# Sigmoid attention and routed tokens: a DRAM-to-DRAM output copy, a reset of the bank order, and a reordered last batch

## The chip, the cores and the metric

The kernel runs on one core of a Trainium2 chip. Its engines are TensorE (PE, matrix products; PEld is its weight load), VectorE (DVE), ScalarE (ACT), GpSimd (POOL) and SyncE (SP, which here issues DMAs and does nothing else). Sixteen DMA engines serve the core. The metric is the device time of one execution in microseconds (us); smaller is better.

## What is computed

Eight batches, 12 heads, 448 tokens, head size 64. First comes attention with a sigmoid in place of the softmax. Its result, laid out as 448 rows of 768 numbers for each batch, goes into a layer in which only 128 of the 448 tokens are routed through two matrix products; the others pass unchanged.

```python
scores = scale * np.matmul(q, k.transpose(0, 1, 3, 2)) - np.log(S)
attn = 1.0 / (1.0 + np.exp(-scores))
x = np.matmul(attn, v)                 # (B,H,S,D) -> (B, S, H*D)
...
scores = np.einsum('bsd,d->bs', x, w_gate)
out = x.copy()
for b in range(B):
    top_idx = np.argpartition(-scores[b], capacity)[:capacity]   # 128 rows
    xe = x[b, top_idx]
    ye = np.maximum(xe @ w1, 0.0) @ w2                           # F = 1024
    g = 1.0 / (1.0 + np.exp(-scores[b, top_idx]))
    out[b, top_idx] = x[b, top_idx] + g[:, None] * ye
```

So every row of `out` is either a row of `x`, or a row of `x` plus a gated product. All numbers are float32.

## The kernel before

The 96 pairs of batch and head are worked in groups of 4 heads, 3 groups to a batch, and in 12 stages `s` of two groups. A stage has 7 units `n`. A unit (`unit`, L193) is 32 matmul instructions into two PSUM tiles and two sigmoid activations on ScalarE. Between the units, `gap(s, n)` (L442) places everything else by hand: the whole kernel stands under a manual schedule, so program order is the order on each engine and each queue, and the semaphores follow from what reads and writes what.

- **PSUM.** Four tiles of two banks: a pool `psc` of two, which the units use, and `ps_o[0]` and `ps_o[1]`. `banks("o")` (L82) flips `turns[0]` and takes that one of the two; `banks("any")` alternates between `psc` and `o`. The attention outputs of a stage use both: `outs[s] = [banks(0), banks(1)]` (L233). After the last part of the products with V, at unit 2 of the next stage, `take` (L259) transposes them out of PSUM on VectorE into `x_b`, four instructions, first both halves of tile 0 and then both of tile 1 (L255 to L257).
- **Rows to DRAM.** When a batch's third group has been taken, `gates` (L435) calls `store(b)` (L280) at unit 2 (even batches) or 3 (odd ones). It writes `x_b` twice, with four DMAs each: into a DRAM table `x_d` (two buffers), and into `out[b]`. `x_b` holds 32 columns of a head to a piece, so that these DMAs move pieces of 128 bytes.
- **Routing.** `spread`, `rank` and `place` find the 128 chosen tokens. `select` and `fetch` (L334, L341), a stage later, turn them into a list of rows (`row`, `idx`, two buffers each) and gather these rows from `x_d` into `xe` by an indirect DMA on POOL (L349). `turn_rows` (L354) transposes them on TensorE. Then follow six routed groups in the list `ready`: three `ffn1` (36, 36 and 24 matmuls, Relu by ScalarE into `hT`) and three `ffn2` (16 matmuls, a third of the columns each, VectorE adds them into `xe`). The last `ffn2` scatters `xe` over `out` with an indirect DMA on POOL (L390). Its destination is named as the whole of `out`, so it is ordered behind every write of `out` that stands before it in the program, and every later write of `out` behind it.
- **Where they go.** `go` pops one group from `ready`; `gap` calls it at units 3, 4 and 5. `late` holds what is due at a place (`put`, `due`); `beside` holds the selects.
- **The end.** Stage `NS` = 12 has only gaps. Batch 6 is chosen, five gaps run, three more groups are popped, batch 7 is chosen (`choose(B - 1)`, L504), the rest of `ready` is popped (L505), and then come `turn_rows` and the six groups of batch 7.

SP issues in program order the loads of q and k (`load`, L90), of v (`load_v`, L100), the weights, and the stores.

Of the kernel before, what the change touches and what calls it, by code (L numbers as in the profile page):

```python
# [17 lines left out]
def kernel(  # L18
# [11 lines left out]
    nc = tc.nc  # L30

    B, H, S, Dh = q.shape
# [4 lines left out]
    TT = 32  # L37
    TB = S // TT
# [35 lines left out]
    turns = [0, 0]  # L74
# [15 lines left out]
    def load(i):  # L90

        if i >= NQ:
            return
        raws[i] = [raw.tile([P, TB * Dh], F32, name=f"raw_{nm}") for nm in "kq"]
        for t, src in zip(raws[i], (k, q)):
            nc.sync.dma_start(
                out=t, in_=bass.AP(tensor=src.tensor, offset=src.offset + i * 4 * S * Dh,
                                   ap=[[TB * Dh, P], [1, TB * Dh]]))
# [76 lines left out]
    def turn(i):  # L175


        if i >= NQ:
            return
        kT[i] = head.tile([P, 2, TB, TT], F32, name="kT")  # L180
        qT[i] = head.tile([P, 2, TB, TT], F32, name="qT")
        sk, sq = [t.rearrange("p (r e d) -> p e r d", e=2, d=TT) for t in raws.pop(i)]
        for e in range(2):
            nc.vector.transpose(kT[i][:, e, :HK],  # L184
                                sk[:, e, :HK].rearrange("p (m c) d -> p c m d", c=NF))
        nc.vector.transpose(kT[i][:, :, HK:], sk[:, :, HK:])
        if i == 0:
            for e in range(2):
                nc.vector.transpose(qT[i][:, e], sq[:, e])
        else:  # L190
            nc.vector.transpose(qT[i], sq)  # L191
# [33 lines left out]
    x_tiles, gate_parts, st = {}, {}, {}  # L225
    def values(s, n):

        tv, th = raw_v[s]
        if n == 0:
            outs[s] = [banks(0), banks(1)]  # L233
        o = outs[s]
        first = (0, 2, 2, 0)[n]
        quads = [(first + m) % 4 for m in range(4)]
        work = [(r, c) for c in range(NF) for r in quads]
        if n < 2:
            at = 4 * (NF - 1)
            work[at:at] = [(r, None) for r in quads]  # L240
        for r, c in work:
            x, pr = divmod(r ^ n, 2)
            rows = slice(r * TT, (r + 1) * TT)
            for j in range(2):
                if c is None:
                    w, a = th[rows, 2 * pr + j, :], attn[s, pr, NF]
                else:
                    w = tv[rows, 4 * x + 2 * pr + j, c * Dh:(c + 1) * Dh]
                    a = attn[s, pr, (NF + 1) * x + c]
                nc.tensor.matmul(o[x][j * Dh:(j + 1) * Dh, pr, :S], w, a[rows, j, :],  # L250
                                 start=(n == 0 and c == 0), stop=(n == 3 and c == NF - 1))
        if n < 3:
            nc.scalar.activation(o[x][Dh:Dh + 1, pr, S:S + 1], bias_s[Dh:Dh + 1], AF.Copy)  # L253
        else:
            for x in range(2):  # L255
                for pr in range(2):
                    take(s, pr, x)  # L257
# [11 lines left out]
    def gate_part(i):  # L269
        b, g = divmod(i, NG)  # L270
        tmp = moe.tile([P, TB, 2 * TT], F32, name="scr")
        nc.vector.tensor_tensor(  # L272
            out=tmp,
            in0=x_tiles[b][:, :, 2 * g:2 * g + 2, :].rearrange("p r h d -> p r (h d)"),
            in1=wg_b[:, 2 * g:2 * g + 2, :].rearrange("p (o h) d -> p o (h d)", o=1)
            .to_broadcast([P, TB, 2 * TT]),
            op=ALU.mult)
        nc.vector.tensor_reduce(out=gate_parts[b][:, :, g], in_=tmp, axis=AX.X, op=ALU.add)  # L278

    def store(b):  # L280
        x_d = dram.tile([S, D], F32, name="x_d")
        st[b] = dict(x_d=x_d)
        for dst in (x_d, out[b]):
            view = dst.rearrange("(t r) (h a d) -> a t r h d", r=TB, a=4, d=TT)
            for a in range(4):
                nc.sync.dma_start(out=view[a], in_=x_tiles[b][a * TT:(a + 1) * TT])

    def gate(b):
        g = moe.tile([P, TB], F32, name="gate_s")
        nc.vector.tensor_reduce(out=g, in_=gate_parts[b], axis=AX.X, op=ALU.add)  # L290
        diag = moe.tile([P, TB, TT], F32, name="rep")
        nc.vector.tensor_tensor(
            out=diag,
            in0=iden_t.rearrange("p (o t) -> p o t", o=1).to_broadcast([P, TB, TT]),
            in1=g.rearrange("p (r o) -> p r o", o=1).to_broadcast([P, TB, TT]), op=ALU.mult)
        st[b]["diag"] = diag
# [37 lines left out]
    def select(b, s0, n, pk):  # L334

        tg = tok_gate[b % 2]
        for c in range(NC):
            nc.tensor.matmul(pk[:n, 0:2], sel[:, c, s0:s0 + n], tg[:, c, :],
                             start=(c == 0), stop=(c == NC - 1))
# [56 lines left out]
    ready = []  # L396
# [7 lines left out]
    def go(where="o"):  # L404
        if ready:
            fn, args = ready.pop(0)
            fn(*args, where)

    late = {}
    beside = {}  # L410

    def put(where, s, n, fn, *args):
        where.setdefault((s, n), []).append((fn, args))

    def due(where, s, n):
        for fn, args in where.pop((s, n), []):
            fn(*args)

    def routed(b):

        s = (NG * b + NG - 1) // 2 + 1
        put(late, s, 5 if b == 0 else 4, spread, b)
        for c in range(NC - 1):
            put(late, s, 6 if b == 0 else 4, rank, b, c)
        put(late, s, 6, rank, b, NC - 1)
        put(late, s, 6, place, b)
        if s == NS:
            return
        for s0, n in SLOTS:
            if s + 1 < NS:  # L430
                put(beside, s + 1, 1 if b == 0 else 0, select, b, s0, n)
            put(late, s + 1, 3, turn_rows, b, n)
            put(late, s + 1, 3, routed_groups, b, n)

    def gates(i):  # L435
        gate_part(i)
        b, g = divmod(i, NG)
        if g == NG - 1:
            store(b)
            gate(b)  # L440

    def gap(s, n):  # L442
        if n < 3 and s > 0:
            values(s - 1, n + 1)
            if n == 2:
                gates(2 * s - 2)
        if 3 <= n < NU - 1:
            if not ready:
                due(late, s, n)
            go("any" if s == NS else "o")  # L450
            if n == NU - 2 and s < NS - 2 and len(ready) > 1:
                go()
        if n == NU - 1 and s < NS:
            values(s, 0)
        due(late, s, n)
        if n == 3 and s > 0:
            gates(2 * s - 1)

    def stream():
        for b in range(B):  # L460
            routed(b)
        load(0)
        load(1)
        nc.vector.memset(sel, 0.0)
        nc.vector.memset(bias_s, NEG_LOG_S)
        turn(0)
        load(2)
        load_v(0)
        warm = banks(1)
        for _ in range(3):  # L470
            nc.tensor.matmul(warm[:, 0], sel[:, 0, :], sel.rearrange("p c n -> p (c n)"),
                             start=True, stop=True)
        constants()
        for s in range(NS):
            for n in range(NU):
                unit(s, n)
                if n == (0 if s == 0 else 1):
                    turn(2 * s + 1)
                    load(2 * s + 3)
                if n == 0:  # L480
                    load_v(s + 1)
                    load_weights(5 * s - 5, 5 * s)
                if s == 0 and n == 1:
                    nc.vector.tensor_reduce(
                        out=iden_t, in_=iden.rearrange("p (a t) -> p t a", t=TT),
                        axis=AX.X, op=ALU.add)
                gap(s, n)
                if n == NU - 2:
                    turn(2 * s + 2)
                    load(2 * s + 4)  # L490

        def choose(b):
            for s0, n in SLOTS:
                pk = banks("psc")[:, 0]
                select(b, s0, n, pk)
                fetch(b, s0, n, pk)

        choose(B - 2)
        for n in range(5):
            gap(NS, n)  # L500
        for n in range(3):
            go("any")
        due(late, NS, NU - 1)
        choose(B - 1)  # L504
        while ready:  # L505
            go("any")
        for s0, n in SLOTS:
            turn_rows(B - 1, n, "any")
            routed_groups(B - 1, n)
        while ready:  # L510
            go("any")
        assert not late and not beside
# [32 lines left out]
```

## Time and profile before

| | us |
|---|---|
| time, median of 3 runs | 503.19 (501.88 to 513.16) |
| the profiled execution, its own time | 502.38 |
| its span, first to last instruction | 500.6 |
| PE busy in it | 473.4 (95%) |
| DVE, ACT, POOL busy | 211.8, 189.3, 28.0 |
| mean granted TensorE clock | 0.986 of full speed |
| DMA queue of SP, share of 16 engines' span | 55.9% |

The profile is of one execution. A row of a timeline gives the start and the length in us, the engine, the line of the kernel, the operation, what it writes and reads, the number of instructions merged into the row, and in brackets how long the engine had been idle before it and what released it. The start of one row of matmuls to the start of the next is the pitch: matmuls overlap, and their lengths add up to more than the time they take.

### The profile page before, as it was taken

How to read it: one execution, taken by the hardware profiler on the slowest of the kernel's cores; microseconds unless marked ns; L12 is line 12 of the kernel's file. 1: busy time of each engine (PE TensorE's matmuls, PEld its weight loads, DVE VectorE, ACT ScalarE, POOL GpSimd, SP SyncE). 2: the span in 40 equal slices, each digit the busy share in tenths (PEclk: the TensorE clock that was granted, in tenths of full speed). 3: DMA queues.
4: the chain of work that ended last, by engine and by line, in shares of the span. 5: the costliest groups of instructions: out<-in, count | busy, mean ns of one | idle time of the engine just before them, and what ended most of it. 6: DMA issues, size and time to landing. Idle time of an engine off the chain costs nothing. (4 is left out here: it accounts for less than half of the span.)

```text
span 500.6 us, 14613 instructions
## 1 busy us (share of the span) xinstructions
PE 473.4 (95%) x6662; PEld 307.7 (61%) x6662; DVE 211.8 (42%) x461; ACT 189.3 (38%) x253; POOL 28.0 (6%) x45
## 2 busy tenths in 40 slices
PE   8998999599999999999999999999999999996995
PEld 3564646476477465576467476567565475685894
DVE  4324295526351167345343066257154146470101
ACT  4754464232542543442533442444443443000010
POOL 8000000000000000010000000010000000000100
PEclk9998999799999999999999999999999999999899
DMA  8929198898791097898453098597650077284100
GB/s 268 224 70 352 51 317 128 174 306 132 156 211 75 20 198 128 196 206 133 127 130 106 5 202 130 145 232 121 157 148 33 3 116 118 49 129 98 56 8 31
DMA packets 203421, 68.67 MB, mean 137 GB/s; under 512 B 182048, under 2 KB 194400, under 8 KB 203360
## 3 DMA queue, kind: packets, MB, share of 16 engines
q1 hardware_dynamic: 201952, 61.36, 55.9%
q0 software_dynamic: 1408, 6.39, 4.1%
q8 instruction: 52, 0.85, 0.8%
q14 instruction: 9, 0.07, 0.0%
HBM read 42.57 MB, written 25.17 MB: 135 GB/s over the span
## 5 line engine op out<-in xcount | busy, mean ns | idle before, releaser
L220 ACT ACTIVATE attn<-psc,bias_s 128x896 f32<-128x896 f32 x158 | 151.1, 1003 | 129.8 <-PE psc L209 116.4
L209 PE MATMUL psc<-qT,kT 32*64 32x448 f32 x2528 | 149.4, 545 | 1.4 <-ACT attn L220 1.4
L250 PE MATMUL o<-attn,raw_v 32*64 32x448 f32 x2304 | 133.9, 539 | 0.8 <-ACT o L253 0.8
L209 PEld LDWEIGHTS psc<-qT,kT 32*64 32x64 f32 x2528 | 60.1, 132 | 62.1 <-issue 41.3
L250 PEld LDWEIGHTS o<-attn,raw_v 32*64 32x64 f32 x2304 | 58.8, 133 | 50.3 <-issue 41.9
L375 PEld LDWEIGHTS o<-xeT,w_sb 128*128 128x128 f32 x672 | 78.8, 197 | 12.9 <-issue 6.4
L375 PE MATMUL o<-xeT,w_sb 128*128 128x128 f32 x672 | 81.6, 282 | 3.1 <-DVE x_b L265 2.2
L384 PE MATMUL o<-w_sb,hT 128*128 128x256 f32 x304 | 70.4, 386 | 4.3 <-DVE x_b L265 4.3
L265 DVE STREAM_TRANSPOSE x_b<-o 128x448 f32<-128x448 f32 x48 | 26.9, 617 | 109.2 <-PE o L250 86.7
L384 PEld LDWEIGHTS o<-w_sb,hT 128*128 128x128 f32 x304 | 57.1, 192 | 21.0 <-PE psc L209 7.3
L184 DVE STREAM_TRANSPOSE kT<-raw_k 128x384 f32<-128x384 f32 x48 | 24.7, 553 | 29.0 <-PE psc L209 15.9
L386 DVE SCALAR_TENSOR_TENSOR xe<-o,gate,xe 128x256 f32<-128x256 f32 x19 | 9.2, 483 | 55.4 <-PE o L384 55.4
L377 ACT ACTIVATE hT<-o 128x384 f32<-128x384 f32 (+1 forms) x21 | 9.5, 454 | 57.2 <-PE o L375 57.2
L250 PE MATMUL o<-attn,raw_h 32*64 32x448 f32 x384 | 26.4, 535 | 0.0
L278 DVE TENSOR_REDUCE gate_p<-scr 128x14 f32<-128x896 f32 x24 | 26.1, 1087 | 0.8
L272 DVE TENSOR_TENSOR scr<-x_b,wg_b 128x896 f32<-128x896 f32 x24 | 25.6, 1066 | 0.1
L191 DVE STREAM_TRANSPOSE qT<-raw_q 128x896 f32<-128x896 f32 x23 | 24.7, 1073 | 1.2 <-DMA raw_q<-in_q_dram 1.2
L349 POOL DMA_INDIRECT xe<-x_d,row x8 | 7.9, 988 | 297.0 <-DVE idx L345 221.2
L384 PE MATMUL psc<-w_sb,hT 128*128 128x256 f32 x80 | 19.4, 395 | 4.5 <-ACT hT L377 4.5
L322 DVE SCALAR_TENSOR_TENSOR scr<-rep,tok_gate,earlier 128x448 f32<-128x448 f32 (+1 forms) x32 | 21.8, 682 | 1.1
L319 DVE TENSOR_SCALAR_CACHE_REDUCE scr<-rep,tok_gate 128x448 f32<-128x448 f32 (+1 forms) x32 | 21.4, 669 | 0.9
L307 DVE STREAM_TRANSPOSE scr<-o 128x448 f32<-128x448 f32 x8 | 5.2, 650 | 37.2 <-ACT rep L305 37.2
(54 smaller groups left out, 199.9 us busy)
## 6 DMA issues: line engine op xcount, KB each, us to landing
raw_k<-in_k_dram SPq DMA_DIRECT2D x24, 448.0 KB, 5.0
raw_q<-in_q_dram SPq DMA_DIRECT2D x24, 448.0 KB, 5.5
x_d<-x_b SPq DMA_DIRECT2D x32, 336.0 KB, 7.2
out_dram<-x_b SPq DMA_DIRECT2D x32, 336.0 KB, 6.8
raw_v<-in_v_dram SPq DMA_DIRECT2D x48, 192.0 KB, 4.4
w_sb<-in_moe_w_dram SPq DMA_DIRECT2D x6, 512.0 KB, 5.9
w_sb<-in_moe_w_dram SPq DMA_DIRECT2D x8, 384.0 KB, 4.7
raw_h<-in_v_dram SPq DMA_DIRECT2D x48, 32.0 KB, 4.5
```

The source lines that it names most:

```text
L184: nc.vector.transpose(kT[i][:, e, :HK], sk[:, e, :HK].rearrange("p (m c) d -> p c m d", c=NF))
L191: nc.vector.transpose(qT[i], sq)
L209: nc.tensor.matmul(psc[h // 2][y * Dh:(y + 1) * Dh, h % 2, :S], kT[2 * s + x][d, e, r:r + 2, :].rearrange("d r t -> d (r t)"), qT[2 * s + ...
L220: nc.scalar.activation(a, psc[pr][:, :, :S], AF.Sigmoid, bias=bias_s, scale=QK_SCALE)
L250: nc.tensor.matmul(o[x][j * Dh:(j + 1) * Dh, pr, :S], w, a[rows, j, :], start=(n == 0 and c == 0), stop=(n == 3 and c == NF - 1))
L265: nc.vector.transpose(x_tiles[b][:, :, 2 * g + pr, :], outs[s][x][:, pr, :S].rearrange("p (r t) -> p r t", t=TT))
L272: nc.vector.tensor_tensor(out=tmp, in0=x_tiles[b][:, :, 2 * g:2 * g + 2, :].rearrange("p r h d -> p r (h d)"), in1=wg_b[:, 2 * g:2 * g + 2 ...
L278: nc.vector.tensor_reduce(out=gate_parts[b][:, :, g], in_=tmp, axis=AX.X, op=ALU.add)
L319: nc.vector.tensor_scalar(out=junk[:n], in0=rep[:n], scalar1=own, scalar2=0.0, op0=ALU.is_gt, op1=ALU.add, accum_out=above[:n, c:c + 1])
L322: nc.vector.scalar_tensor_tensor(out=junk[:n], in0=rep[:n], scalar=own, in1=earlier[:n, c, :], op0=ALU.is_equal, op1=ALU.mult, accum_out=l ...
L375: nc.tensor.matmul(ps[:, f - f0, :n], w1_sb[:, t, f * P:(f + 1) * P], xeT[:, t, :n], start=(t == 0), stop=(t == KD - 1))
L384: nc.tensor.matmul(ps[:n, :ND], st[b]["hT"][:, t, :n], w2_sb[:, t, cols], start=(t == 0), stop=(t == KF - 1))
```

## The change

There are four edits. `store` writes only the table `x_d`. A new `copy_out(b)` copies the whole table of a batch into `out[b]` by one DMA, DRAM to DRAM, on SP; it is put at unit 1 of stage 3 for batch 0, at unit 6 of the stage of the store for batches 1 to 6, and right behind `choose(B - 1)` for batch 7. `gap` sets `turns[0]` to 1 at unit 2 of each stage after the first, so that the next `banks("o")` takes tile 0. At the end, the last group of batch 6 (its third `ffn2`, with the scatter) stands behind `turn_rows` of batch 7 rather than ahead of it.

```diff
     def store(b):
         x_d = dram.tile([S, D], F32, name="x_d")
         st[b] = dict(x_d=x_d)
-        for dst in (x_d, out[b]):
-            view = dst.rearrange("(t r) (h a d) -> a t r h d", r=TB, a=4, d=TT)
-            for a in range(4):
-                nc.sync.dma_start(out=view[a], in_=x_tiles[b][a * TT:(a + 1) * TT])
+        view = x_d.rearrange("(t r) (h a d) -> a t r h d", r=TB, a=4, d=TT)
+        for a in range(4):
+            nc.sync.dma_start(out=view[a], in_=x_tiles[b][a * TT:(a + 1) * TT])
+
+    def copy_out(b):
+        nc.sync.dma_start(out=out[b], in_=st[b]["x_d"])
...
         put(late, s, 6, place, b)
         if s == NS:
             return
+        put(late, *((s + 1, 1) if b == 0 else (s, 6)), copy_out, b)
...
             values(s - 1, n + 1)
             if n == 2:
+                turns[0] = 1
                 gates(2 * s - 2)
...
         due(late, NS, NU - 1)
         choose(B - 1)
-        while ready:
+        copy_out(B - 1)
+        while len(ready) > 1:
             go("any")
         for s0, n in SLOTS:
             turn_rows(B - 1, n, "any")
```

## Rows read from the trace of the kernel before

**Rows 1.** The page: busy time of each engine, share of the span, instructions.
```profile
PE 473.4 (95%) x6662; PEld 307.7 (61%) x6662; DVE 211.8 (42%) x461; ACT 189.3 (38%) x253; POOL 28.0 (6%) x45
```

**Rows 2.** Waits of PE: line, released by; us in total, times, longest.
```profile
PE o L359 <- DMA xe<-x_d,row: 4.7, 1, 4.7
PE psc L384 <- ACT hT L377: 4.5, 1, 4.5
PE o L384 <- DVE x_b L265: 4.3, 4, 1.1
PE o L375 <- DVE x_b L265: 2.2, 2, 1.1
```

**Rows 3.** Timeline of VectorE and PE, one of the six waits on L265.
```profile
173.36 2.24 DVE L265 STREAM_TRANSPOSE x_b<-o 128x448 f32<-128x448 f32 x4 [12.91 <-PE o L250]
...
175.75 2.92 PE L375 MATMUL o<-xeT,w_sb 128*128 128x128 f32 x24 [1.09 <-DVE x_b L265]
```

**Rows 4.** Timeline of PE, the last 65 us.
```profile
435.10 0.82 PE L359 MATMUL o<-iden,xe 128*128 128x128 f32 x6
435.75 3.62 PE L384 MATMUL o<-w_sb,hT 128*128 128x256 f32 x16
...
455.58 2.76 PE L384 MATMUL psc<-w_sb,hT 128*128 128x256 f32 x12
...
473.75 4.29 PE L375 MATMUL psc<-xeT,w_sb 128*128 128x128 f32 x36 [0.64 <-ACT xeT L362]
...
488.03 3.62 PE L384 MATMUL psc<-w_sb,hT 128*128 128x256 f32 x16
491.48 3.62 PE L384 MATMUL o<-w_sb,hT 128*128 128x256 f32 x16
```

**Rows 5.** Timeline of VectorE, POOL and ScalarE around the last routing.
```profile
446.94 0.48 DVE L386 SCALAR_TENSOR_TENSOR xe<-psc,gate,xe 128x256 f32<-128x256 f32 x1
...
453.00 0.16 DVE L343 CAST row<-psc 128x1 int32<-128x1 f32 x1 [3.18 <-PE psc L338]
...
459.04 0.99 POOL L390 DMA_INDIRECT out_dram<-xe,idx  x1 [34.99 <-DMA out_dram<-x_b]
462.10 0.16 DVE L345 TENSOR_SCALAR idx<-psc 128x1 int32<-128x1 f32 x1 [8.94 <-DMA out_dram<-xe,idx]
...
462.42 0.38 ACT L377 ACTIVATE hT<-o 128x256 f32<-128x256 f32 x1
```

**Rows 6.** SP's timeline, stores of batch 7; below, their landing from issue.
```profile
434.08 8.87 SPq L286 DMA_DIRECT2D x_d<-x_b  x4
442.99 10.56 SPq L286 DMA_DIRECT2D out_dram<-x_b  x4
...
DMA to landing us min/median/max: 6.4/6.5/7.6
```

**Rows 7.** Timelines of SP, POOL and PE, batch 0; then stretch, busy, PEclk, DMA.
```profile
69.12 13.39 SPq L286 DMA_DIRECT2D x_d<-x_b  x4
...
88.15 1.11 POOL L349 DMA_INDIRECT xe<-x_d,row  x1 [75.78 <-DMA x_d<-x_b]
...
93.88 1.41 PE L359 MATMUL o<-iden,xe 128*128 128x128 f32 x6 [4.66 <-DMA xe<-x_d,row]
...
93.90:101.00 7.10, 6.20 (x29) 5.80 (x30) 1.33 (x3) 0.81 (x1) 0.00 (x0) 0.52 0.89 207
```

**Rows 8.** Line L349, all eight gathers: from issue to landing.
```profile
DMA to landing us min/median/max: 3.8/5.5/6.6
```

**Rows 9.** Busiest stretch of the DMA engines: last two columns, DMA share and GB/s.
```profile
43.00:47.00 4.00, 4.00 (x63) 1.97 (x55) 0.40 (x1) 1.36 (x2) 0.00 (x0) 0.60 1.02 417
```

**Rows 10.** Timeline of POOL: gather of batch 2, scatter of 1, gather of 3.
```profile
198.80 0.98 POOL L349 DMA_INDIRECT xe<-x_d,row  x1 [50.52 <-DVE idx L345]
215.15 1.58 POOL L390 DMA_INDIRECT out_dram<-xe,idx  x1 [15.38 <-DVE xe L386]
238.93 0.97 POOL L349 DMA_INDIRECT xe<-x_d,row  x1 [22.20 <-DVE idx L345]
```

## The prediction, made before the result was seen

> **What bounds the kernel.** I read the page first: PE is busy 473.4 of 500.6 us, and no other engine comes to half the span [rows 1]. The kernel is bound by TensorE, and a change that takes no matmul away can win only the 27.2 us in which PE stands idle, and the time for which its clock is down. DMA traffic, which this change cuts most, wins nothing by itself: what counts is a wait of PE that ends with a DMA. So the second view is PE's waits. Four lines of it hold 15.7 us [rows 2]: one wait of 4.7 us for a gather, one of 4.5 us for ScalarE's `hT`, and six of 1.1 us for the transposes at L265. The rest of the idle time is the start, the end (from 495.1, the end of the last matmul, to 500.6; [rows 4]) and small waits. The timelines then say what stands behind each of the three kinds, and in the windows I looked for clock loss behind them.
>
> **Bank order (`turns[0] = 1`).** The four transposes of a stage take 2.24 us, so a pair takes 1.12, and tile 0's pair comes first. In the stage shown they start at 173.36: tile 0 is free at 174.48, tile 1 at 175.60. PE was ready at 175.75 - 1.09 = 174.66 and had to wait for tile 1 [rows 3]. Had its first routed group asked for tile 0, it would have found it free 0.18 us before it was ready; the small delay behind a semaphore (0.15 us here, 175.60 to 175.75) about eats that, so the wait comes to 0 and not below. This pattern stands six times (stages 5, 6, 7, 9, 10 and 11), 4.3 + 2.2 = 6.5 us [rows 2]. In the other stages the flip happened to stand right already. What is late next: the stage's second request goes to tile 1, which is free 1.0 us after PE's new start (175.60 against 174.66); it comes after the first group, 16 matmuls or more, 3.45 us at the shortest (the pitch in rows 4). So nothing follows, and I take **-6.5 us**. Bounds: 0 if the wait merely moves, -6.5 if it goes.
>
> **The end of the kernel.** Here the second store costs time. Follow rows 5 backwards. PE stops within the first `ffn2` of batch 6, for `hT`. The third part of `hT` is written by ScalarE only at 462.42, since it stands there behind the gate activation of `fetch(7)`, which needs `idx` on VectorE. That was ready to go at about 453.2, behind the cast at 453.00, but waited 8.94 us: it overwrites the buffer of batch 5, which the scatter of batch 5 still reads. The scatter's data were ready at 446.94 + 0.48 = 447.4, but it is ordered behind all earlier writes of `out`, and the store of `out[7]` (four DMAs, issued from 442.99 to 453.55, landing 6.4 to 7.6 us after their issue [rows 6]) was one of them. Hence POOL starts only at 459.04, and `idx` follows 3.06 us later at 462.10 [rows 5].
>
> After the change the write of `out[7]` stands behind `choose(7)` in the program. The scatter of batch 5 goes at 447.5 and has landed at about 450.6, ahead of the cast at 453.00; `idx`, gate and `hT` are not held. Then the last group of batch 6 stands behind `turn_rows(7)`, and its 3.46 us of matmuls cover the eviction for which PE waits 0.64 us now (the row at 473.75). In sum: from the start of the first `ffn2` (455.58) to the start of batch 7's `ffn1` (473.75) it takes 18.17 us now. The same matmuls at undisturbed pitch are three `ffn2` at 491.48 - 488.03 = 3.45 and one `turn_rows` at 435.75 - 435.10 = 0.65 us, together 11.0 [rows 4]. That takes in the stall of 4.5, the 0.64, and the half-speed clock after the stall. **-7.1 us.**
>
> **The copies.** One copy reads and writes 1.376 MB. No DRAM-to-DRAM transfer is in the trace. Its bounds: at the rate of the busiest stretch, 417 GB/s [rows 9], 3.3 us; at that of the four stores it replaces, 10.56 us of issue plus 6.5 of landing [rows 6], 17 us. Its rows are 3 KB, nearer to the loads of that stretch than to pieces of 128 bytes; reading and writing DRAM both count, so I double the lower one and add 3 for the landing: about 9 us, an estimate.
>
> [...]
>
> Each copy adds two waits on SP: for the landing of its `x_d`, and for earlier scatters. Behind it on SP stand loads of v, q and k for a stage later, which already wait for buffers. Each copy also adds a wait on POOL: the next scatter must see it landed. The tightest of these in mid-kernel is the copy of batch 2 (put a few us ahead of the gather at 198.80) against the scatter at 215.15 [rows 10], 16 us or more. For batch 7, SP reaches the copy when `x_d` has landed (issue over at 442.95, so about 449.5 at the latest) and the scatter of batch 5 has (450.6): the copy runs from about 451 to 460. What waits for it is the scatter of batch 6, now due at about 467, and behind it that of batch 7 at 495.9 - 7.1 = 488.8. I take 0 for the copies.
>
> What the copy may hold up is `fetch(7)`, which issues at about 453.4. A gather takes 3.8 to 6.6 us, the most beside loads and stores [rows 8]; it lands between 457.2 and 460. `turn_rows(7)` comes after two more `ffn2`, at 455.58 + 6.9 = 462.5. Slack 2.5 us at worst: 0.
>
> **Batch 0.** [...] PE was ready at 89.22. The stores of `x_d(0)` are unchanged, and end at 82.5; landing at 6.4 at best after the last issue (about 79.9) would free the gather at about 86.5, against 88.15. Beside it then run the loads of group 8 and of v, now earlier by the 11 us of the second store, in its place. So the gather lands between 86.5 + 3.8 = 90.3 and 88.15 + 6.6 = 94.8, against 93.8: a gain of 3.5 to a loss of 1. Nearer to today's than to a free queue, so I take **-1.0 us**; the clock falls as now.
>
> **Sum.** 502.38 (the profiled execution's own time) - 6.5 - 7.1 - 1.0 = 487.8. The median of the runs is 0.8 above that execution, so I say **488 us**, 3.0% less. What a measurement can tell from no change is about 2%, here 10 us: the line is 493.1.
>
> **Rivals.**
> - *The gather of batch 0 escapes.* If it lands by 90.3, the wait falls to 1.1 us, a length after which none of the six shows more than its wait. Then also the clock stays: 7.1 us at 0.52 lose 3.4. 487.8 + 1.0 - 3.6 - 3.4 = 481.8; at most about 480.5. For it: the 128-byte pieces behind `x_d` go. Against: loads take their place. Chance 0.08.
> - *The copy of batch 7 holds up `fetch(7)`.* With the copy at its upper price the two share the engines until 451 + 17 = 468, and `turn_rows(7)` waits up to 5.5 us from 462.5, with about 1.6 us of lower clock behind it: up to 7.1 back, 489 to 495. Decides when the gather needs over 9.1 us. Against: 6.6 is the longest seen. Chance 0.13.
> - *The bank waits stay.* If a tile's release counts the reads of both tiles, or another user takes tile 0 first, 6.5 comes back: 494. Against: PE's start 0.15 us behind the fourth transpose in rows 3, and stages without the wait. Chance 0.09.
> - *Slower: the copy runs on one DMA engine.* One sixteenth of 417 is 26 GB/s, 53 us a copy. Batch 2's would run from about 195 to 248, the scatter of 1 to 252, and VectorE, in order, would hold at `idx` of the gather now at 238.93, some 13 us and PE about 10 of them; the same at batch 4. At the end 451 + 53 = 504, then two scatters in a row, 3 and 4.7 us to the end of the span: 512 for 500.6, less the 7.5 gained before, plus 20 and the 1.8 outside the span, about 526. It decides only where a copy takes over some 34 us (485 for the scatter of 6, to be out of the way at 488.8), so not at two engines, 26 us. For it: no row shows such a transfer; against: SP's loads keep all sixteen engines busy (share 1.02 in rows 9). Chance 0.05.
>
> [...]
>
> **Chances.** Forecast 0.65 (486 to 490 by itself), rivals as given. Leaving out the slower one and most of the unforeseen, the range is 480.5 to 495. Faster by over 2%: 0.65 + 0.08 + half of the held gather, 0.79. Within: the rest of that and the bank rival, 0.16. Slower: 0.05.
>
> **What would show it.** Right: no wait of PE on L265 at the routed groups; POOL's scatter of batch 5 within a us of VectorE's `xe`; no wait of PE on `hT`, no clock below full in the last 40 us; `ffn1` of batch 7 about 7 us closer to the first `ffn2`; a wait on the first gather of 3 to 4.7 us still there. Wrong: copies that land later than 17 us after issue; a wait of PE at `turn_rows(7)`; POOL waiting for `out`<-`x_d`.

## The result: 2.5% faster, with a loss at one place where a gain was forecast

The changed kernel takes 489.85 us (median of 4 runs, 488.26 to 490.36), the kernel before beside it 502.53. The ratio is 0.9749, with a 95% interval of 0.9712 to 0.9787. The forecast was 488, with a range of 480.5 to 495. The profiled execution took 489.37 us, with a span of 487.6 for 500.6: 13.0 us less. Ratios here and below compare fast runs alone; one run of the kernel before (513.16 us) and one of the first experiment (974.12 us) were slow ones and are not in them.

The page of the changed kernel, busy times, clock, DMA traffic and the new copies; the last row gives KB and us from issue to landing (for one of the eight copies, the only one whose landing this profile has):

```profile
PE 470.9 (97%) x6662; PEld 309.5 (63%) x6662; DVE 211.7 (43%) x461; ACT 189.4 (39%) x253; POOL 28.0 (6%) x45
...
PEclk9999999789999999999999999999999999999999
...
DMA packets 117277, 68.67 MB, mean 141 GB/s; under 512 B 95648, under 2 KB 108000, under 8 KB 116960
...
q1 hardware_dynamic: 115808, 61.35, 49.0%
...
out_dram<-x_d SPq DMA_DIRECT2D x8, 1344.0 KB, 9.0
```

TensorE does the same 6662 matmuls. What fell is its idle time, from 27.2 to 16.7 us, and, by 2.5 us, its busy time, which is longer where the clock is low: in the window 43 to 46.5 us, shown below, 48 matmuls fill the 3.5 us at a granted clock of 0.54 and 81 at 1.00 (the mean over the span was 0.986 before and is 0.988 here). DMA packets fell by 42% (203421 before), which by itself, as the third experiment shows (128045 packets, ratio 1.0025), shortens the run by nothing. PE's waits, to be laid beside [rows 2]:

```profile
PE o L361 <- DMA xe<-x_d,row: 5.9, 1, 5.9
PE psc L209 <- ACT attn L220: 1.9, 2, 1.4
...
PE o L377 <- ACT xeT L367: 0.9, 1, 0.9
...
```

The six waits on L265 and the wait for `hT` are gone. The wait for the first gather is not only still there, it grew from 4.7 to 5.9 us.

**Bank order.** The stage of [rows 3] in the timelines of VectorE and PE:

```profile
173.12 2.24 DVE L265 STREAM_TRANSPOSE x_b<-o 128x448 f32<-128x448 f32 x4 [12.88 <-PE o L250]
...
174.45 2.92 PE L377 MATMUL o<-xeT,w_sb 128*128 128x128 f32 x24
```

The group starts 1.33 us after the first transpose, when the first pair (1.12 us) is out and the second is not; before, it started 2.39 us after it. No idle time stands beside the row.

**The end.** Timelines of PE, POOL, VectorE, ScalarE and SP, to be laid beside [rows 4 to 6]:

```profile
428.33 8.86 SPq L285 DMA_DIRECT2D x_d<-x_b  x4
...
441.19 0.48 DVE L388 SCALAR_TENSOR_TENSOR xe<-psc,gate,xe 128x256 f32<-128x256 f32 x1
...
441.95 0.99 POOL L392 DMA_INDIRECT out_dram<-xe,idx  x1 [23.55 <-DVE xe L388]
...
445.01 0.53 SPq L288 DMA_DIRECT2D out_dram<-x_d  x1
...
447.33 0.15 DVE L347 TENSOR_SCALAR idx<-psc 128x1 int32<-128x1 f32 x1
447.68 0.97 POOL L351 DMA_INDIRECT xe<-x_d,row  x1 [4.75 <-DVE idx L347]
...
449.84 3.62 PE L386 MATMUL psc<-w_sb,hT 128*128 128x256 f32 x16
...
450.04 0.38 ACT L379 ACTIVATE hT<-o 128x256 f32<-128x256 f32 x1 [2.29 <-PE o L377]
...
460.86 4.18 PE L377 MATMUL psc<-xeT,w_sb 128*128 128x128 f32 x36
```

The scatter of batch 5 goes 0.3 us after its data; `idx` follows the cast at once; the last part of `hT` is begun 0.2 us after the first `ffn2` and done at 450.42, before that `ffn2` comes to it. From that `ffn2` to batch 7's first `ffn1` it takes 460.86 - 449.84 = 11.02 us, for 18.17 before.

**Batch 0.** Timelines of SP, POOL and PE, and the window behind the wait (PE busy, PEclk, DMA share, GB/s), to be laid beside [rows 7]:

```profile
67.77 13.41 SPq L285 DMA_DIRECT2D x_d<-x_b  x4
81.70 2.17 SPq L96 DMA_DIRECT2D raw_k<-in_k_dram  x1
...
86.12 1.81 SPq L115 DMA_DIRECT2D raw_v<-in_v_dram  x4
...
86.54 1.11 POOL L351 DMA_INDIRECT xe<-x_d,row  x1 [74.18 <-DMA x_d<-x_b]
...
85.57 1.95 PE L209 MATMUL psc<-qT,kT 32*64 32x448 f32 x32
93.42 1.51 PE L361 MATMUL o<-iden,xe 128*128 128x128 f32 x6 [5.90 <-DMA xe<-x_d,row]
...
102.39 1.76 PE L209 MATMUL psc<-qT,kT 32*64 32x448 f32 x32
...
93.40:101.00 7.60, 6.68 (x31) 0.51 1.06 406
```

In the place of the second store, loads of k, q, v and `w2` run beside the gather. It lands 6.7 us after its issue, at 93.3, where it took 5.6 us in the kernel before; and the clock is low behind the wait, 0.51 for 0.52 there.

**Where the 13.0 us lie.** Two units frame batch 0. For the kernel before they, and a window 50 us earlier, stand here:

```profile
87.27 1.94 PE L209 MATMUL psc<-qT,kT 32*64 32x448 f32 x32
...
102.61 1.76 PE L209 MATMUL psc<-qT,kT 32*64 32x448 f32 x32
...
43.00:46.50 3.50, 3.50 (x48) 0.54 1.02 417
```

And the same window of the changed kernel:

```profile
43.00:46.50 3.50, 3.50 (x81) 1.00 1.03 414
```

| stretch, us | before | changed | difference |
|---|---|---|---|
| start to the unit ahead of `turn_rows(0)` | 87.27 | 85.57 | -1.70 |
| from it to the unit behind the first `ffn1` | 15.34 | 16.82 | +1.48 |
| from there to the first `ffn2` of the end | 352.97 | 347.45 | -5.52 |
| from it to `ffn1` of batch 7 | 18.17 | 11.02 | -7.15 |
| from there to the end of the span | 26.85 | 26.74 | -0.11 |

The first row is not what the change was made for. 1.7 us of it are the clock in the window 43 to 46.5: from a unit at 36 us to one at 62 us it takes 26.51 us before (36.01 to 62.52) and 24.82 in the changed kernel (36.45 to 61.27). This goes with the execution and not with the edit: the first experiment, on the changed kernel, has 26.51 there (clock 0.52 from 44 to 46 us), and the second, on the kernel before, 24.83 (1.00). Of the seven profiles of the experiments four have the low clock (0.50 to 0.56 from 44 to 46 us) and three have not (1.00). What is left of the row cancels: the changed kernel is 0.44 us later ahead of that window and 0.45 us sooner behind it. The 0.45 may belong to the change, since from the unit at 62 us to the one ahead of `turn_rows(0)` all seven kernels with copies take 24.30 us, and the two without 24.75 and 24.67; where it comes from is not shown. The two programs are not quite the same up to there either: the reset acts from stage 1 on, and a wait of 0.50 us for ScalarE at L302 has become one of 0.45 at L209.

In the third row the six waits are gone, 6.5 us, of which 1.0 is missing. It belongs to this execution and not to the edit: from the gather of batch 5 to the scatter of batch 4, and on to the gather of batch 6, it takes 27.25 and 39.49 us; the profile of the sixth experiment, where these stages are the same, has 26.59 and 39.08, the kernel before less its two waits 26.59 and 39.07.

### The profile page after: what moved, and what is told of

Read it like the earlier page. It is cut to its first block, busy times and chain, and to the rows that moved or that the text cites. A ratio compares the mean times of both kernels' runs of the same rounds, so it can differ in the third digit from the quotient of the medians.

```text
span 487.6 us, 14593 instructions
## 1 busy us (share of the span) xinstructions
PE 470.9 (97%) x6662; PEld 309.5 (63%) x6662; DVE 211.7 (43%) x461; ACT 189.4 (39%) x253; POOL 28.0 (6%) x45
## 2 busy tenths in 40 slices
DMA packets 117277, 68.67 MB, mean 141 GB/s; under 512 B 95648, under 2 KB 108000, under 8 KB 116960
## 4 chain that ended last, share of the span: by engine, by line
PE 85%; issue 4%; DMA 3%; DVE 3%; SPq 2%; ACT 1%; POOLq 0%; DVEq 0%; ACTq 0%
PE o L250 24%; PE psc L209 24%; PE o L377 16%; PE o L386 13%; SPq L285 2%; PE o L209 2%; DMA x_d<-x_b 1%; PE psc L386 1%; DMA xe<-x_d,row 1%; PE psc L340 1%; PE o L304 1%; PE o L361 1%; PE o L475 1%; DVE x_b L265 1%; PE psc L377 1%
## 5 line engine op out<-in xcount | busy, mean ns | idle before, releaser
L209 PE MATMUL psc<-qT,kT 32*64 32x448 f32 x2528 | 150.3, 540 | 1.9 <-ACT attn L220 1.9
L209 PEld LDWEIGHTS psc<-qT,kT 32*64 32x64 f32 x2528 | 61.5, 131 | 61.1 <-issue 37.4
L250 PEld LDWEIGHTS o<-attn,raw_v 32*64 32x64 f32 x2304 | 60.3, 132 | 48.6 <-issue 38.8
L386 PE MATMUL o<-w_sb,hT 128*128 128x256 f32 x320 | 73.4, 383 | 0.0
L265 DVE STREAM_TRANSPOSE x_b<-o 128x448 f32<-128x448 f32 x48 | 26.9, 618 | 106.9 <-PE o L250 83.7
L386 PEld LDWEIGHTS o<-w_sb,hT 128*128 128x128 f32 x320 | 59.4, 190 | 16.8 <-issue 5.8
L253 ACT ACTIVATE o<-bias_s 1x1 f32<-1x1 f32 x36 | 5.9, 165 | 36.8 <-PE o L250 24.9
```

What stands on the lines that cost most here:

```text
L209: nc.tensor.matmul(psc[h // 2][y * Dh:(y + 1) * Dh, h % 2, :S], kT[2 * s + x][d, e, r:r + 2, :].rearrange("d r t -> d (r t)"), qT[2 * s + ...
L265: nc.vector.transpose(x_tiles[b][:, :, 2 * g + pr, :], outs[s][x][:, pr, :S].rearrange("p (r t) -> p r t", t=TT))
L386: nc.tensor.matmul(ps[:n, :ND], st[b]["hT"][:, t, :n], w2_sb[:, t, cols], start=(t == 0), stop=(t == KF - 1))
```

## The experiments

**Is it the bank order that takes the six waits away?**

```diff
             if n == 2:
-                turns[0] = 1
                 gates(2 * s - 2)
```

> The changed kernel without the reset of the bank order. If the six waits on the transposes at L265 went because the first routed group of a stage now asks for tile 0, they are back, up to six of 1.1 us, and the time is 6.5 us above the changed kernel's 489.9: about 496.4. If they went because there is less DMA traffic, or because the end was reordered, they stay away and the time stays within 1 us of 489.9. The end of the kernel, from the first ffn2 of batch 6 to ffn1 of batch 7, keeps its 11.0 us under both.

497.31 us (median of 4), ratio 0.9887 (0.9857 to 0.9916), which is 0.0138 above the changed kernel's, 6.9 us. PE's waits of this kernel:

```profile
PE o L361 <- DMA xe<-x_d,row: 6.0, 1, 6.0
PE o L386 <- DVE x_b L265: 4.4, 4, 1.1
PE o L377 <- DVE x_b L265: 2.2, 2, 1.1
```

All six are back, 6.6 us, though the DMA traffic is that of the changed kernel, and the end keeps its length (457.73 to 468.75, 11.02 us). The line of code is the cause.

**Is it the order of the writes of `out`, or the traffic, that held up the end?** In the kernel before, only the place of the last store is changed.

```diff
-        for dst in (x_d, out[b]):
+        for dst in (x_d, out[b])[:1 if b == B - 1 else 2]:
...
         choose(B - 1)
+        view = out[B - 1].rearrange("(t r) (h a d) -> a t r h d", r=TB, a=4, d=TT)
+        for a in range(4):
+            nc.sync.dma_start(out=view[a], in_=x_tiles[B - 1][a * TT:(a + 1) * TT])
```

> The kernel before, with one edit: the four old stores of out[7], SBUF to DRAM in 128-byte pieces, stand behind choose(7); everything else is as before. If the wait for hT at the end comes from the order of the scatter of batch 5 behind the write of out[7], it is gone without any copy: 18.17 us from the first ffn2 to ffn1 of batch 7 become about 11.7 (the 0.64 us wait for the eviction of turn_rows stays), and the time falls by 6.4 us to about 496. If it is the length or the traffic of the stores that costs, and the gain came from the copy being shorter, PE waits as long at turn_rows(7) and the time stays at 502.5.

496.91 us, ratio 0.9887 (0.9865 to 0.9910): 5.7 us less than before, with an interval wholly below 1, and without a copy. Timelines of SP and PE:

```profile
450.38 9.34 SPq L507 DMA_DIRECT2D out_dram<-x_b  x4
...
455.20 3.62 PE L384 MATMUL psc<-w_sb,hT 128*128 128x256 f32 x16
...
467.02 4.29 PE L375 MATMUL psc<-xeT,w_sb 128*128 128x128 f32 x36 [0.64 <-ACT xeT L362]
```

The stretch takes 467.02 - 455.20 = 11.82 us, with the 0.64 of `turn_rows` still in it. The old stores are issued up to 459.72, within this stretch, and hold up nothing in it.

**What do the copies do by themselves?** In the kernel before, batches 0 to 6 are copied, and everything else stays.

```diff
-        for dst in (x_d, out[b]):
+        for dst in (x_d, out[b])[:2 if b == B - 1 else 1]:
...
+        put(late, *((s + 1, 1) if b == 0 else (s, 6)), copy_out, b)
```

> The kernel before, with the copies in place of the second store for batches 0 to 6 only; the last batch, the bank order and the end are as before. If less DMA traffic wins nothing by itself, the share of SP's DMA queue falls from 56% to about 50%, but the time does not fall: it stays at 502.5, or rises by about 1.5 us if the gather of batch 0 is slower beside the loads that move up into the place of the second store (wait at L359 near 5.9 us in place of 4.7, gather landing 6.7 us after issue in place of 5.6). If that longer wait in the changed kernel was only a difference from run to run, the wait is 4.7 or less here. If the traffic matters to TensorE, the time falls by more than 2 us.

504.25 us (10 runs), ratio 1.0025 (0.9999 to 1.0050). The page and PE's waits:

```profile
q1 hardware_dynamic: 126576, 61.35, 48.3%
...
PE o L362 <- DMA xe<-x_d,row: 6.4, 1, 6.4
PE psc L387 <- ACT hT L380: 4.7, 1, 4.7
```

The queue's share falls by 8 points, and the time does not. The wait for the first gather is 6.4 us for 4.7; the gather lands 7.4 us after issue. So the longer wait does not need the reset or the new end: it belongs to the copies, or to what moves up because of them. It was 5.7 to 6.4 us in each of the five profiles with the loads in that place, and 4.5 and 4.7 in the two with the second store there.

**What makes the first gather slow?** The loads are moved away from it, behind the store of batch 1.

```diff
+                if (s, n) == (3, 3):
+                    load(8)
+                    load_v(4)
+                    load_weights(10, 15)
+                    load(9)
+                    copy_out(0)
```

(Each of these is left out at its old place.)

> The changed kernel, with the loads of groups 8 and 9, of v for stage 4, the last four of w2 and the copy of batch 0 all moved behind the store of batch 1 (stage 3, unit 3). SP holds at that store until VectorE has transposed, at about 88, so nothing of SP's is issued beside the first two us of the gather of batch 0, and then 128-byte pieces. If the gather of batch 0 takes 6.7 us in the changed kernel because the loads run beside it, it lands at most 4.5 us after issue here, still issued at 86 to 86.5 (the stores of its table are unchanged); the wait of PE at turn_rows(0) falls from 5.9 to 3 to 4 us, and the time by about 2 us to 488. If the gather is slow for another reason (its table has just been written), it still takes 6 us or more and the time stays at 490. If a load now comes too late, PE shows a wait behind stage 3 and the time is above 490.

487.72 us, ratio 0.9720 (0.9691 to 0.9749). Timelines of POOL and PE, and the gather's landing from issue:

```profile
88.01 1.11 POOL L351 DMA_INDIRECT xe<-x_d,row  x1 [75.65 <-DMA x_d<-x_b]
...
92.19 1.51 PE L361 MATMUL o<-iden,xe 128*128 128x128 f32 x6 [2.98 <-DVE gate_p L278]
...
DMA to landing us min/median/max: 4.0/4.0/4.0
```

The table has just been written here too, and the gather takes 4.0 us for 6.7. Nearly nothing runs beside it (DMA share 0.35 from 84 to 90 us): the stores of batch 1 begin some 2 us after it. PE's wait falls to 2.98 us (it is put down to VectorE, whose last event before it came at about the same time; 88.01 + 4.0 = 92.0 is the gather). The time against the changed kernel, 0.0029 or 1.5 us by the two ratios, lies within their intervals; the row is what decides. PE waits 0.6 us for `w2` in this order.

**And can the wait be taken away?** The table of batch 0 is stored behind 1.57 MB of `w2`; these four loads are put a stage later.

```diff
-                    load_weights(5 * s - 5, 5 * s)
+                    load_weights(*{1: (0, 5), 2: (5, KD), 3: (KD, KD + KF)}.get(s, (0, 0)))
```

> The changed kernel with the eight loads of w2 all at the start of stage 3, four of them a stage later than now: x_d(0) is then stored behind 1.57 MB less of loads. If the gather of batch 0 is late because its table is stored behind these loads, the stores of x_d(0) take 9 to 11 us to issue in place of 13.4, the gather starts about 4 us earlier, the wait of PE at turn_rows(0) falls from 5.9 us to 0 to 2, and the clock does not fall behind it: 5 to 9 us less than the changed kernel, 481 to 485. If the stores are slow by themselves (128-byte pieces), the gather starts at most 1 us earlier and the time stays at 488 to 490. If the first ffn2 comes to wait for w2, PE shows that wait on L129's DMAs, and the time is above 490.

483.27 us (481.60 to 483.86), ratio 0.9617 (0.9595 to 0.9640): 1.3% below the changed kernel, and the fastest of all. Timelines of SP, POOL and PE, then PE's wait:

```profile
66.53 10.05 SPq L285 DMA_DIRECT2D x_d<-x_b  x4
...
81.66 1.12 POOL L351 DMA_INDIRECT xe<-x_d,row  x1 [69.26 <-DVE idx L347]
...
87.99 0.88 PE L361 MATMUL o<-iden,xe 128*128 128x128 f32 x6
...
PE o L377 <- ACT xeT L367: 1.9, 1, 1.9
```

The stores issue in 10.05 us for 13.41, and the gather no longer waits for them at all, but for `idx`. It has landed before PE comes to it. No low clock follows (1.00 from 84 to 98 us); the mean over the span is 0.998. What remains is the eviction behind `turn_rows(0)`, for which PE waits 1.9 us.

**What does moving the last group win?**

```diff
-        while len(ready) > 1:
+        while ready:
             go("any")
```

> The changed kernel with the last group of batch 6 ahead of turn_rows(7) again, as it was before. If moving it only covers the eviction behind turn_rows, PE waits 0.64 us there again and the stretch from the first ffn2 of batch 6 to ffn1 of batch 7 takes 11.7 us in place of 11.0. If the order also matters for the gather of batch 7, PE waits longer at turn_rows(7) here or not at all in both.

One run, 488.53 us; a difference of half a us can't be read from that, but the timeline of PE can be:

```profile
448.09 3.62 PE L386 MATMUL psc<-w_sb,hT 128*128 128x256 f32 x16
...
459.91 4.29 PE L377 MATMUL psc<-xeT,w_sb 128*128 128x128 f32 x36 [0.64 <-ACT xeT L364]
```

11.82 us, for 11.02 with the group moved: 0.8, the eviction's 0.64 and the gaps at it.

**Is it then the place alone?** The copy of batch 7 stands ahead of the scatter of batch 5 again, as the old store did.

```diff
         if s == NS:
+            put(late, NS, 4, copy_out, b)
             return
...
-        copy_out(B - 1)
```

> The changed kernel with the copy of batch 7 put ahead of the scatter of batch 5 in the program (stage 12, unit 4), as the old store was; the copy itself is the same. If the place in the order is what costs at the end of the kernel, the scatter of batch 5 waits for the copy (table landed at about 443.5, plus 9 us), so it goes at about 453 in place of 442, idx follows at about 456, and PE waits 3 to 4.5 us for hT: with the clock behind it 4 to 6.5 us above the changed kernel, 494 to 496. If the copy being one DMA of large pieces is what wins there, the time stays within 1 us of 489.9.

487.70 us, ratio 0.9712 (0.9686 to 0.9739). The first expectation failed: the time did not rise. Timelines of SP, POOL, VectorE, ScalarE and PE, and the copy's landing:

```profile
441.82 0.53 SPq L288 DMA_DIRECT2D out_dram<-x_d  x1
...
448.66 0.99 POOL L392 DMA_INDIRECT out_dram<-xe,idx  x1 [29.70 <-DVE row L345]
...
450.39 3.62 PE L386 MATMUL psc<-w_sb,hT 128*128 128x256 f32 x16
...
451.71 0.16 DVE L347 TENSOR_SCALAR idx<-psc 128x1 int32<-128x1 f32 x1 [3.75 <-DMA out_dram<-xe,idx]
...
452.03 0.38 ACT L379 ACTIVATE hT<-o 128x256 f32<-128x256 f32 x1
...
DMA to landing us min/median/max: 6.0/6.0/6.0
```

The chain that I named is there, link by link: the scatter waits from 442.2 (its data, 441.74 + 0.48) to 448.66 (its row names VectorE's cast, which ended at 447.97; the copy landed at about the same time, 441.82 + 6.0 = 447.8), `idx` waits 3.75 us for it, and `hT` comes at 452.41. But that is in time. The last four matmuls of the `ffn2` that began at 450.39 need it, about three quarters of 3.45 us later, at 453.0. My numbers for two links were too large: the table had landed by 441.82 (I had 443.5), and the copy, with nothing beside it, in 6.0 us (I had 9). So the place is not the only way. The copy of 6 us in the old place, or the old store (9.34 us of issue alone) behind the scatter, each takes the stall away, the first with 0.6 us to spare; the changed kernel has both, and needs one.

## Why the prediction was right, and where it was not

- **Bank order, -6.5: right.** Six waits gone, six back without the line (6.6 us). That the next request finds tile 1 free was right too: no row of L265 is left in PE's waits.
- **The end, -7.1: right in size** (-7.15 in the profile), and each link as foretold. The half-speed clock that the step counts is 0.50 from 462.8 to 466 us in the kernel before; in the changed kernel the clock is 1.00 from 428 to 462. It was too narrow in its cause: I credited the place of the write alone. The second experiment shows that the place suffices, the last one that the shorter write does as well. In the same step I counted the landing of `x_d(7)` from the end of the issue of four DMAs, not from the issue of the last; the copy was ready sooner than the "449.5 at the latest", and waited for the scatter only, as the rows of SP show (445.01, which is 441.95 + 3.06).
- **The copies at 0: right for what waits for them.** About 9 us was the estimate; 9.0 is the one landing in this profile, and the profile of the last experiment has 6.0 to 8.7 for seven of its eight copies. For the copy of batch 7 the view of the DMA queues (444 to 456 us; q1 with packets, MB, share) has

```profile
DMA packets 176, 1.98 MB, mean 165 GB/s; under 512 B 48, under 2 KB 48, under 8 KB 143
...
q1 hardware_dynamic: 48, 1.38, 31.6%
```

  Of these packets 33 hold 8 KB or more, one of them on the queue for instructions: the copy's 1.376 MB went in 32 packets of 43 KB, so the rows of 3 KB on which I had costed it were not what the engines saw, and neither the doubling nor the 3 us rested on a row: they were my own estimate, and no run shows the doubling. The rival with one DMA engine, 53 us, is out: the landings seen were 6.0 to 9.0 us. So is that of a held `fetch(7)`: it took 5.4 us, within the gathers of [rows 8], and landed 3.7 us before `turn_rows(7)` at 456.75.
- **Batch 0, -1.0: wrong in sign.** This is the step that failed; it measured +1.5 in this pair of profiles. The other four profiles with the loads in that place take 15.79 to 16.70 us for the stretch, the second experiment, with the old store in it, 14.99; so the sign holds, and the size is some 1.3 us in the mean.

  Two things went into the -1.0. I took 1.65 us for an earlier start of the gather, from 88.15 to 86.5, by counting 6.4 us from the issue of the table's last store (79.9) to the gather. But my own rows have 88.15 - 79.9 = 8.3 us there, and in the changed kernel the gather gained 0.3: from the first store to it it takes 86.54 - 67.77 = 18.77 us, for 19.03 in [rows 7]. Against PE, which is what makes the wait (it was ready at 93.88 - 4.66 = 89.22 in [rows 7]), it gained nothing: it starts 0.97 us after the unit ahead of `turn_rows(0)`, for 0.88 before. The second thing is what -1.0 leaves for a slower gather, 0.65 us; the loads lengthened it by 1.1, from 5.6 to 6.7 us. I had named these loads, and their direction, and still took a value on the other side of zero. The wait of 3 to 4.7 us that I gave as a sign of being right was missed as well, at 5.9. The fourth experiment, with 4.0 us, shows what either neighbour costs: 1.6 us the stores, 2.7 the loads.
- **The rival of batch 0** (481.8) had its direction right: in the fifth experiment the gather landed before PE came, 4.2 us after its issue, and the wait and the low clock behind it were both gone (1.00 from 84 to 98 us). It took that edit to get there: 483.27. That the clock stays up after a wait of 1.1 us, as the rival had it, no run tested at this place; after the 2.98 us of the fourth experiment it was down (0.50 from 94 to 98 us).
- **The sum** of 487.8 lay 1.6 us under the profiled execution. 2.5 of that is the term of batch 0, and 1.0 is what is missing in the third row of the table; the first row, 1.7, which no term foresaw, and 0.2 of smaller ones go the other way. The 1.0 and the 1.7 belong to the two executions and not to any reason in the forecast, so that the total came this near is in part luck. With the 0.8 us between that execution and the median the sum should have read 488.6 and not 488; the median is 489.85.

## What to carry to other kernels

Where one engine is 95% busy, ask what a change to the DMA traffic does to the waits of that engine: here about half of the packets under 512 bytes went (182048 before, 95648 after), and where only the copies were put in, the time did not fall (ratio 1.0025). List these waits, and ask of each which transfer ends it. In this kernel an indirect write that names a whole tensor is ordered against every write of that tensor (the scatter of batch 5 waited for the store of `out[7]`, [rows 5]): keep bulk writes of it short, or behind the scatter in program order, above all where buffers that the scatter reads come round again. And the store taken out of SP's queue did not leave a hole: the next loads in the queue moved up, and became the neighbours of a gather on another queue, which took 6.7 us for 5.6.

## What the runs showed of the hardware

- A gather of 128 rows of 3 KB took 3.8 us with nothing beside it (batch 7 of the kernel before), 4.0 with nearly nothing (batch 0 of the fourth experiment), 5.6 and 6.0 beside stores in pieces of 128 bytes (batches 0 and 1 of the kernel before), and 6.6 to 7.4 beside loads of k, q, v and `w2` (batch 0 in five profiles).
- A DRAM-to-DRAM copy of 1.376 MB landed 6.0 us after issue with nothing beside it (batch 7 of the last experiment); the longest in that profile was 8.7 us, and the one landing in the changed kernel's is 9.0. At the end of the changed kernel it went in 32 packets of 43 KB. The four stores that it replaces took 10.56 us to issue alone.
- After the same wait of 1.4 us at 40 to 42 us the granted clock was 0.50 to 0.56 from 44 to 46 us in five of the nine profiles, and 1.00 in the other four. It is 1.7 us of noise (26.51 us for 24.82 from the unit at 36 us to the one at 62) that a comparison of two profiles has to take out first.
